# Zeroed tiles in one memset, shared K semaphores, a 16-slot last piece of V, and the final scale on VectorE, in a single-core decode attention kernel

## The chip, the cores and the metric

The kernel runs on one core of a Trainium2 chip. The metric is device time of one execution in microseconds (us), lower is better. The engines are called TensorE (PE in the profile), VectorE (DVE), ScalarE (ACT), GpSimd (POOL) and SyncE (SP); the last one issues nearly all the loads here. Unless a text says otherwise, a position is counted from the start of the profiled span; where several runs are compared in one table it is counted from the issue of the first load of K, which comes 0.95 to 0.96 us later.

## The reference

Single-token attention over a long cache: 32 query heads share 8 heads of K and V, each of 65536 keys by 128 values, all in bf16.

```
B, Hq, Hkv, Sq, Sk, D = 1, 32, 8, 1, 65536, 128
scores = einsum("bhqd,bhkd->bhqk", q, repeat(k, 4)) * D ** -0.5
p      = softmax(scores)
out    = einsum("bhqk,bhkd->bhqd", p, repeat(v, 4))
```

K and V together are 268 MB, and the output is 8 KB. Each byte is used once.

## The kernel before

For each of the G = 8 K/V heads, K and V come in two blocks of 256 "slots" (a slot is one key for each of 128 partitions: 32 KB). VectorE transposes K in place, TensorE makes the scores, ScalarE the exponentials, and TensorE multiplies them with V. The last block of V comes in pieces, at the slot numbers in CUTS.

```python
SL, TAIL, P, D, G, H = 256, 32, 128, 128, 8, 4
CUTS = [0, 128, 192, 224, 232, 240, 248, 252, 256]

def wait(self, *waits):              # Queue.wait, line 37 of the profile's listings
    for sem, n in waits:
        if n > 0:
            self.eng.wait_ge(sem, n)
...
    ex = sb("ex", [P, 4, 512], bf16)      # exponentials
    vs = sb("vs", [P, D + 2], fp32)       # sums that the last gather adds up over partitions
    vy = sb("vy", [P, D, 4], fp32)
...
    GP.mark(gp.memset(wz[:, :, :], 0.0))
    GP.mark(gp.memset(vs[:, :], 0.0))
    GP.mark(gp.memset(ex[:, :, :], 0.0))
    GP.mark(gp.memset(vy[:, :, :], 0.0))
    n = GP.mark(gp.memset(ident[:, :], 0.0))
...
    with block("pe_values"):              # V times exponentials, "wide": 512 columns a matmul
        take(pe, PE, s_et, 1)
        for ch in range(4):
            ...                           # waits for the load of this quarter
            for tt in range(16 if ch < 3 else (SL - TAIL) % PS // 4):
                i = wide(ch, tt)
            ...
            if ch in (1, 2):              # a matmul whose result nobody reads
                pe.matmul(out=pt[0:16, :], lhsT=et[:, 0, 0:16], rhs=et[:, 0, :],
                          start=True, stop=True)
...
    # the end on TensorE: 32 slots as "narrow" matmuls, 128 columns each
    for t in range(SL - TAIL, SL):
        if t in CUTS:
            pe.wait_ge(s_v[CUTS.index(t)], 16)
        if t == CUTS[-2]:
            pe.wait_ge(s_dv, d_last)
            gather(D, start=False, stop=False)      # adds VectorE's sums of all other slots
        w0 = t % PS // 4 * 32 + 16 + 4 * (t % 4)
        i = pe.matmul(
            out=fin, lhsT=et[:, 1, w0:w0 + H], rhs=io[:, t, :], start=(t == SL - TAIL),
            stop=(t == SL - 1), skip_group_check=True,
        )
    i.then_inc(s_pe, 1)
...
    # the end on VectorE and ScalarE
    n = DV.mark(dve.tensor_tensor(
        out=vs[:, 0:D], in0=vz[:, 0, :], in1=vz[:, 1, :], op=ALU.add
    ))
    assert n == d_last
    DV.wait((s_pt, 1))
    d_rl = DV.mark(dve.reciprocal(out=rl[:, :], in_=pl))
    ACTQ.wait((s_dv, d_rl), (s_pe, 1))
    n = ACTQ.mark(act.activation(out=o[:, :], in_=fin, func=ACT.Copy, scale=rl[:, :]))
    ACTQ.after(n)
    act.dma_start(out=out[0, (G - 1) * H:G * H, 0, :], in_=o[:, :]).then_inc(s_st, 16)
    ACTQ.wait((s_st, 32))
```

## Time and profile before

| | before |
|---|---|
| time, median of 3 | 629.61 us (629.51 to 629.65) |
| span of the profiled execution | 627.7 us |
| moved by DMA | 268.49 MB, 428 GB/s over the span |
| busy: TensorE, VectorE | 57%, 55% of the span |
| last piece of V has landed | 624.11 us |
| output DMA issued | 625.28 us |

The page's rows by slice: each digit is the busy share of one of 40 slices of 15.7 us in tenths, PEclk is the clock granted to TensorE in tenths of full speed, and GB/s is what the DMA moved.

```profile
PEclk9978595967959678596785958859587695899676
DMA  8999999999999999999999999999999999999996
GB/s 362 441 468 401 468 401 468 401 468 401 468 401 464 405 459 409 447 422 447 422 438 430 426 443 409 459 405 464 401 468 401 468 401 468 396 437 434 434 432 274
```

The DMA engines are busy at 90% or more in all slices but the first and the last. The kernel is a stream, and only its two ends can be shortened. TensorE's clock moves between half and full speed all the time: the clock record of this trace has 38 stretches at either 0.50 or 1.00, and the mean granted clock of the execution was 0.796.

The chain of waits that ended last, in order of time (start us, us, what; x is a count). Its end:

```profile
609.01 12.42 DMA io<-in_v_dram
621.43 0.04 issue
621.48 1.03 PE acc L254 x6
622.50 0.03 PE pb L348
622.53 1.80 PE pf L359 x28
624.33 0.23 PE pf L248 x2
624.56 0.24 PE pf L359 x4
...
624.82 0.02 ACTq L37
624.84 0.05 issue
624.89 0.36 ACT o L487
```

The chain names the piece of slots 192 to 223 as the last DMA. The trace's records of DMA completions show more: the pieces that begin at slots 192, 224, 232, 240, 248 and 252 had landed at 621.43, 622.11, 622.78, 623.45, 623.78 and 624.11 us. So the 28 narrow matmuls (L359) follow the landings closely, and the gather (L248) starts about when the last piece is there. After the last matmul (end 624.79 us) ScalarE waits (ACTq L37), and takes 0.36 us.

The startup, from the timeline (start us, us, engine, line, operation, out<-in):

```profile
1.52 0.21 POOL L187 MEMSET vs<- 128x130 f32 x1
1.67 1.81 POOL L188 MEMSET ex<- 128x2048 bf16 x1
3.41 0.52 POOL L189 MEMSET vy<- 128x512 f32 x1
...
8.50 4.45 DVE L373 STREAM_TRANSPOSE io<-io 128x4096 uint32<-128x4096 uint32 x1 [1.34 <-DVEq L119]
```

VectorE waits 1.34 us for the first K piece, after everything else of the startup is done.

### The profile page before, as it was taken

What the parts mean: (1) busy time and instruction counts of PE and PEld (TensorE: products, weight loads), DVE (VectorE), ACT (ScalarE), POOL (GpSimd) and SP (SyncE); (2) the same over time, 40 slices, a digit from 0 to 9 for tenths busy, and PEclk for the clock granted to TensorE, in tenths of its full rate; (3) what the DMA queues carried; (4) which work ended last, traced back from release to release, by engine and by line L of the source; (5) the groups of instructions that cost most, each with busy time, mean ns of one, the idle gap of its engine ahead of it and who ended that gap; (6) DMA issues with size and microseconds to landing.
All of it is one profiled execution on the core that took longest, in us unless ns stands there. A gap on an engine that the chain in (4) does not pass through costs nothing. (4 is left out here: it accounts for less than half of the span.)

```text
span 627.7 us, 7067 instructions
## 1 busy us (share of the span) xinstructions
PE 356.4 (57%) x2142; PEld 139.8 (22%) x2142; DVE 345.5 (55%) x154; ACT 34.4 (5%) x26; POOL 9.7 (2%) x42
## 2 busy tenths in 40 slices
PE   1865483827638275381844808458193571886346
PEld 0322131312213032130321303123031230332112
DVE  7795835649066490764807557084670946684210
ACT  0000100020000200002000020000200002000100
POOL 2000000000000000000000000000000000000000
PEclk9978595967959678596785958859587695899676
DMA  8999999999999999999999999999999999999996
GB/s 362 441 468 401 468 401 468 401 468 401 468 401 464 405 459 409 447 422 447 422 438 430 426 443 409 459 405 464 401 468 401 468 401 468 396 437 434 434 432 274
DMA packets 7003, 268.49 MB, mean 428 GB/s; under 512 B 856, under 2 KB 1112, under 8 KB 1496
## 3 DMA queue, kind: packets, MB, share of 16 engines
q1 hardware_dynamic: 6944, 268.45, 99.2%
q8 instruction: 1, 0.02, 0.0%
q14 instruction: 2, 0.02, 0.0%
q10 hardware_dynamic: 56, 0.01, 0.0%
HBM read 268.44 MB, written 0.01 MB: 428 GB/s over the span
## 5 line engine op out<-in xcount | busy, mean ns | idle before, releaser
L301 PE MATMUL acc<-io,wz 128*128 x1024 | 272.7, 420 | 184.8 <-PEq L119 157.3
L373 DVE STREAM_TRANSPOSE io<-io 128x4096 uint32<-128x4096 uint32 x64 | 279.9, 4416 | 157.2 <-DVEq L119 157.2
L301 PEld LDWEIGHTS acc<-io,wz 128*128 x1024 | 106.4, 104 | 351.2 <-issue 272.5
L254 PE MATMUL acc<-io,et 128*16 128x512 bf16 x1016 | 72.5, 416 | 19.3 <-PEq L119 19.2
L440 ACT ACTIVATE ex<-acc,nmb 128x2048 bf16<-128x2048 f32 x8 | 15.7, 1967 | 556.9 <-DVE nmb L420 556.9
L410 DVE TENSOR_REDUCE mg<-acc 128x1 f32<-128x2048 f32 x8 | 18.3, 2291 | 48.3 <-DVEq L119 48.3
L254 PEld LDWEIGHTS acc<-io,et 128*16 128x16 bf16 x1016 | 27.7, 94 | 58.4 <-issue 35.5
L248 PE MATMUL pf<-vs,sel 128*4 128x130 f32 (+1 forms) x20 | 5.7, 386 | 54.2 <-PEq L119 54.2
L376 DVE STREAM_TRANSPOSE et<-ex 128x1024 bf16<-128x1024 bf16 x17 | 20.8, 1225 | 22.6 <-SPq L154 12.8
L450 ACT ACTIVATE acc<-wz 128x2560 f32<-128x2560 bf16 (+2 forms) x8 | 16.3, 2040 | 1.0 <-ACT ex L440 0.2
L412 DVE TENSOR_REDUCE m<-pt 1x4 f32<-1x128 f32 x8 | 2.2, 279 | 22.7 <-DVEq L119 22.7
L514 POOL COPY wz<-qT 32x16 bf16<-32x16 bf16 x32 | 6.1, 189 | 512.6 <-PE acc L301 440.3
L248 PEld LDWEIGHTS pf<-vs,sel 128*4 128x4 f32 x20 | 1.2, 83 | 54.7 <-issue 54.6
L326 PE MATMUL pt<-et 128*16 128x512 bf16 x32 | 13.1, 411 | 0.0
L384 DVE TENSOR_REDUCE vs<-vy 128x128 f32<-128x512 f32 x9 | 6.1, 681 | 7.6 <-DVEq L119 7.6
L423 DVE TENSOR_TENSOR vy<-acc,sely 128x512 f32<-128x512 f32 x8 | 8.5, 1064 | 0.0
L472 DVE TENSOR_TENSOR vy<-acc,sely 128x512 f32<-128x512 f32 x1 | 0.7, 691 | 11.5 <-PE acc L254 11.5
L343 PE MATMUL pb<-ident,nrow 1*128 1x1 f32 x8 | 1.6, 194 | 7.5 <-PEq L119 7.5
L326 PEld LDWEIGHTS pt<-et 128*16 128x16 bf16 x32 | 3.1, 97 | 4.5 <-issue 1.4
L341 PE MATMUL pt<-ident,mg 128*1 128x128 f32 x8 | 2.3, 283 | 2.6 <-PEq L119 2.6
L420 DVE COPY nmb<-pb 128x1 f32<-128x1 f32 x8 | 1.3, 157 | 3.9 <-DVEq L119 3.9
L343 PEld LDWEIGHTS pb<-ident,nrow 1*128 1x128 f32 x8 | 1.1, 139 | 8.9 <-issue 8.9
(31 smaller groups left out, 22.8 us busy)
## 6 DMA issues: line engine op xcount, KB each, us to landing
io<-in_v_dram SPq DMA_DIRECT2D x5, 4096.0 KB, 16.9
io<-in_k_dram SPq DMA_DIRECT2D x8, 2048.0 KB, 27.4
io<-in_k_dram SPq DMA_DIRECT2D x2, 4096.0 KB, 34.4
io<-in_v_dram SPq DMA_DIRECT2D x1, 2048.0 KB, 10.3
io<-in_v_dram SPq DMA_DIRECT2D x1, 1024.0 KB, 12.4
io<-in_v_dram SPq DMA_DIRECT2D x3, 256.0 KB, 12.8
io<-in_v_dram SPq DMA_DIRECT2D x2, 128.0 KB, 12.8
io<-in_k_dram SPq DMA_DIRECT2D x13, 48.4
```

Of the source, the lines that this page charges most:

```text
L248: return pe.matmul(out=pf[0:H, 0:w], lhsT=sel[:, :], rhs=vs[:, 0:w], skip_group_check=True, **kw)
L254: return pe.matmul(out=vacc[32 * c:32 * c + 16, :, :], lhsT=et[:, ch // 2, w0:w0 + 16], rhs=io[:, PS * ch + 4 * tt:PS * ch + 4 * tt + 4, : ...
L301: i = pe.matmul(out=bass.AP(acc, r_o, [[2560, P], [1, 512]]), lhsT=bass.AP(wz, r_w + ((2 * s + e) * WB - 4 * u), [[4 * WB, P], [1, P]]), r ...
L326: pe.matmul(out=pt[0:16, :], lhsT=et[:, 0, 0:16], rhs=et[:, 0, :], start=True, stop=True)
L373: dve.transpose(out=part, in_=part).then_inc(s_kt, 2)
L376: dve.transpose(out=et[:, :, :].rearrange("p i n -> p (i n)"), in_=ex[:, 2 * b:2 * b + 2, :].rearrange("p i n -> p (i n)"),).then_inc(s_et, 1)
L384: DV.mark(dve.tensor_reduce(out=vs[:, 0:D], in_=vy[:, :, :], axis=AX.X, op=ALU.add))
L410: dve.tensor_reduce(out=mg[:, :], in_=sc, axis=AX.X, op=ALU.max).then_inc(s_mg, 1)
L423: dve.tensor_tensor(out=vy[:, :, :].rearrange("p d y -> p y d"), in0=vacc, in1=sely[:, :, None].to_broadcast([P, 4, D]), op=ALU.mult,).the ...
L440: act.activation(out=ex[:, :, :].rearrange("p b n -> p (b n)"), in_=sc, func=ACT.Exp, bias=nmb[:, :], scale=SCALE, accum_out=vs[:, D + g % ...
L450: act.activation(out=part, in_=wz[:, 0, 0:1].to_broadcast([P, part.shape[1]]), func=ACT.Copy).then_inc(s_cl, 1)
L514: gp.tensor_copy(out=wz[r, :, c0:c0 + H].rearrange("p (s w) h -> p s w h", s=2), in_=qTb[r, :, :, g, :],).then_inc(s_w, 1)
```

## The change

The intent is to trim both ends: fewer GpSimd instructions and waits at the start, one piece fewer at the end, and one engine fewer between the last product and the output, since VectorE has the reciprocal already. The sharing of K semaphores and the single allocation save resources more than time.

```diff
-CUTS = [0, 128, 192, 224, 232, 240, 248, 252, 256]
+CUTS = [0, 128, 192, 224, 240, 248, 252, 256]
...
-    ex = sb("ex", [P, 4, 512], bf16)
-    vs = sb("vs", [P, D + 2], fp32)
-    vy = sb("vy", [P, D, 4], fp32)
+    zs = sb("zs", [P, 1024 + 4 * D + D + 2], fp32)
+    ex = zs[:, 0:1024].bitcast(bf16).rearrange("p (b n) -> p b n", n=512)
+    vy = zs[:, 1024:1024 + 4 * D].rearrange("p (d y) -> p d y", y=4)
+    vs = zs[:, 1024 + 4 * D:]
...
     s_k = {(b, lo): sem(f"s_k{b}_{lo}") for b in range(2) for lo in k_lo}
+    for lo in k_lo[1::2]:
+        s_k[1, lo] = s_k[0, lo]
...
-    GP.mark(gp.memset(vs[:, :], 0.0))
-    GP.mark(gp.memset(ex[:, :, :], 0.0))
-    GP.mark(gp.memset(vy[:, :, :], 0.0))
+    GP.mark(gp.memset(zs[:, :], 0.0))
...
-    for s in (s_k[1, 64], s_k[1, 192]):
-        gp.sem_inc(s, 16 * (G - 1))
...
-    ACTQ.wait((s_dv, d_rl), (s_pe, 1))
-    n = ACTQ.mark(act.activation(out=o[:, :], in_=fin, func=ACT.Copy, scale=rl[:, :]))
-    ACTQ.after(n)
+    DV.after(d_rl)
+    DV.wait((s_pe, 1))
+    n = DV.mark(dve.tensor_scalar_mul(out=o[:, :], in0=fin, scalar1=rl[:, :]))
+    ACTQ.wait((s_dv, n))
     act.dma_start(out=out[0, (G - 1) * H:G * H, 0, :], in_=o[:, :]).then_inc(s_st, 16)
...
+            if g == 1:
+                GP.wait((s_sc, 8))
+                for t in k_lo[1::2]:
+                    gp.sem_inc(s_k[0, t], 16 * (2 * G - 2))
             GP.wait((s_sc, 16 * g))
             gp.sem_inc(s_sd, 1)
             if g == 1:
-                for t in k_lo[1:]:
-                    gp.sem_inc(s_k[0, t], 16 * (G - 1))
+                gp.sem_inc(s_k[0, 128], 16 * (G - 1))
```

## The prediction

> **What bounds the kernel now.** The DMA stream. The page moves 268.49 MB; the slice table shows the DMA engines at 90% or more in every slice but the first and the last, and the windows view gives 430 to 440 GB/s from 25 to 600 us, with DMA shares of 0.99 to 1.02. [...] PE (57%) and VectorE (55%) have slack. K loads land 48.4 us and V loads 29.4 us after issue (DMA issues), which is far more than the transfer of one 8.4 MB block (about 19.3 us), so the queue always has a next load: compute in the middle costs nothing. Outside the stream are about 2 us before the first packet and all after the last V landing (about 624.1 of 627.7 us).
>
> **Startup.** The three POOL memsets (0.21, 1.81, 0.52 us) become one of 1666 fp32 columns. From vy (512 columns, 0.52 us) and ident (128, 0.20 us) the slope is about 0.83 ns a column: about 1.5 us. The setup ends about 1 us earlier. Worth nothing: VectorE already idles 1.34 us before the first K transpose (start 8.50 us), which waits for the first K piece.
>
> **Shared K semaphores.** The credits of POOL for the second half of each K now come after the first block's scores. The second K block lands after about 32 us, when those scores are done (about 30 us): 0.
>
> **Last V pieces.** In the trace the pieces of slots 192, 224, 232, 240, 248 and 252 land at about 621.43, 622.11, 622.78, 623.45, 623.78 and 624.11 us. An 8-slot piece takes 0.67 us. Packets of 2 KB took 85 ns and of 8 KB 314, so by interpolation 4 KB takes about 161 ns against 2x85: each engine saves about 0.07 us, and the last piece lands about 0.08 us earlier. But TensorE must now wait for slot 224 until about 622.7 rather than 622.39. Its last 32 narrow matmuls run at 55.5 ns each at full clock (107 ns at the half clock granted before about 622.7). 28 of them from 622.75 end at about 624.3; before, the last gather of the sums started at 624.155. So TensorE, not DMA, becomes the last to arrive: +0.15 us (estimate).
>
> **Final scale.** ScalarE: product done 624.79, start 624.89, 0.358 us, output DMA issue 625.28. VectorE: the 4x130 copy from PSUM took 0.28 us and started 0.044 us after its matmul; the hop to ScalarE's queue costs about 0.04. Issue about 0.37 us after the product in place of 0.49: -0.13 us.
>
> **Sum.** +0.15 - 0.13 = about 0: 629.6 us, range 629.1 to 630.1, almost certainly within 2%.
>
> **What would show it.** One POOL memset of about 1.5 us; first K transpose still at 8.5 us; same GB/s in the middle; last piece landing at most 0.1 us earlier relative to the first load; an idle of TensorE of about 0.35 us before the final narrow matmuls, then 28 of them without a gap, and the gather later by 0.15 us; VectorE scale about 0.28 us.
>
> **What would make it wrong.** The half clock staying on through the last matmuls (28 x 50 ns = 1.4 us); a different stream rate in the middle, 0.1% of which is 0.6 us, more than everything argued here; a slow state.

## The result, and the profile after

| | before | after |
|---|---|---|
| time, median of 6 | 629.63 us (629.46 to 630.68) | 630.61 us (630.30 to 632.59) |
| ratio, 95% interval | | 1.0022 (1.0006 to 1.0038) |

The change was meant to shorten the kernel and made it 1.0 us longer by the medians, which is outside of the predicted range (629.1 to 630.1 us). The six times fall in two groups: 630.30, 630.53, 630.59 and 630.63 us, and 632.32 and 632.59 us. The profiled execution is the one of 632.32 us. Its slices, in the columns of before:

```profile
DMA  8999999999999999999999999999999999999995
GB/s 366 432 466 399 466 399 466 399 466 412 453 424 441 441 424 453 412 461 403 466 399 466 399 466 399 466 399 466 399 466 399 466 399 466 398 433 432 432 426 208
```

The stream is as full as it was. The difference is at the end. The chain after:

```profile
608.75 14.18 DMA io<-in_v_dram
622.93 0.04 issue
622.98 3.15 PE pf L359 x28
626.12 0.43 PE pf L248 x2
626.55 0.44 PE pf L359 x4
626.99 0.03 issue
627.02 0.02 DVEq L37
627.04 0.45 issue
627.49 0.34 DVE o L488
```

Two lines stand out. The 28 narrow matmuls take 3.15 us in one uninterrupted row, where before they took 1.80 us with waits between them. And after the separate wait of VectorE (DVEq L37) there are 0.45 us in which VectorE waits for nothing that the profile shows, where ScalarE had 0.05 us.

The windows view gives the reason for the first line. Columns: window, its length, busy us and count of each engine, then the granted TensorE clock, the DMA share and GB/s. Before:

```profile
623.00:624.00 1.00, 1.00 (x21) 0.93 (x18) 0.93 (x4) 0.00 (x0) 0.00 (x0) 1.00 0.26 70
```

After:

```profile
623.00:624.00 1.00, 1.00 (x11) 1.00 (x12) 0.93 (x3) 0.00 (x0) 0.00 (x0) 0.50 0.18 49
624.00:625.00 1.00, 1.00 (x12) 1.00 (x11) 0.31 (x2) 0.00 (x0) 0.00 (x0) 0.50 0.00 0
```

TensorE ran these matmuls at the half clock (0.50), 0.107 us from start to start where full clock gives 0.056 us. The prediction had named this as a risk. Which clock the end meets differs from one execution to the next: in the clock records of all 18 traces the changes lie on a grid of 3.41 us, and this grid begins 0.06 to 3.32 us after the first instruction (1.56 us in the trace of before, 3.05 us in that of after).

The startup did what was expected, to no avail:

```profile
1.52 1.49 POOL L191 MEMSET zs<- 128x1666 f32 x1
...
8.33 4.45 DVE L373 STREAM_TRANSPOSE io<-io 128x4096 uint32<-128x4096 uint32 x1 [2.10 <-DVEq L121]
```

The memset takes 1.49 us, VectorE is ready earlier, and it waits 2.10 us instead of 1.34 us for the same piece of K.

### The profile page after: what moved, and what is told of

It is laid out like the page before. It is cut to its first block, busy times and chain, and to the rows that moved or that the text cites. A ratio compares the mean times of both kernels' runs of the same rounds, so it can differ in the third digit from the quotient of the medians. Undisturbed runs are those within 1.5% of the kernel's fastest.

```text
span 630.5 us, 7062 instructions
## 1 busy us (share of the span) xinstructions
PE 352.6 (56%) x2142; PEld 139.7 (22%) x2142; DVE 345.8 (55%) x155; ACT 34.1 (5%) x25; POOL 8.8 (1%) x40
## 5 line engine op out<-in xcount | busy, mean ns | idle before, releaser
L301 PE MATMUL acc<-io,wz 128*128 x1024 | 268.3, 413 | 189.9 <-PEq L121 158.7
L301 PEld LDWEIGHTS acc<-io,wz 128*128 x1024 | 104.9, 102 | 353.4 <-issue 274.4
L440 ACT ACTIVATE zs<-acc,nmb 128x2048 bf16<-128x2048 f32 x8 | 15.7, 1967 | 556.8 <-DVE nmb L420 556.8
L248 PE MATMUL pf<-zs,sel 128*4 128x130 f32 (+1 forms) x20 | 6.0, 401 | 53.3 <-PEq L121 53.3
L376 DVE STREAM_TRANSPOSE et<-zs 128x1024 bf16<-128x1024 bf16 x17 | 20.8, 1225 | 22.0 <-SPq L158 12.2
L248 PEld LDWEIGHTS pf<-zs,sel 128*4 128x4 f32 x20 | 1.3, 88 | 53.7 <-issue 53.7
L384 DVE TENSOR_REDUCE zs<-zs 128x128 f32<-128x512 f32 x9 | 6.1, 681 | 7.6 <-DVEq L121 7.6
L423 DVE TENSOR_TENSOR zs<-acc,sely 128x512 f32<-128x512 f32 x8 | 8.5, 1065 | 0.0
L472 DVE TENSOR_TENSOR zs<-acc,sely 128x512 f32<-128x512 f32 x1 | 0.7, 690 | 12.5 <-PE acc L254 12.5
L359 PE MATMUL pf<-io,et 128*4 128x128 bf16 x32 | 3.8, 312 | 0.2 <-DMA io<-in_v_dram 0.2
L359 PEld LDWEIGHTS pf<-io,et 128*4 128x4 bf16 x32 | 3.3, 126 | 0.5 <-DMA io<-in_v_dram 0.3
```

The costliest lines, as they stand in the source:

```text
L248: return pe.matmul(out=pf[0:H, 0:w], lhsT=sel[:, :], rhs=vs[:, 0:w], skip_group_check=True, **kw)
L301: i = pe.matmul(out=bass.AP(acc, r_o, [[2560, P], [1, 512]]), lhsT=bass.AP(wz, r_w + ((2 * s + e) * WB - 4 * u), [[4 * WB, P], [1, P]]), r ...
L359: i = pe.matmul(out=fin, lhsT=et[:, 1, w0:w0 + H], rhs=io[:, t, :], start=(t == SL - TAIL), stop=(t == SL - 1), skip_group_check=True,)
L376: dve.transpose(out=et[:, :, :].rearrange("p i n -> p (i n)"), in_=ex[:, 2 * b:2 * b + 2, :].rearrange("p i n -> p (i n)"),).then_inc(s_et, 1)
L384: DV.mark(dve.tensor_reduce(out=vs[:, 0:D], in_=vy[:, :, :], axis=AX.X, op=ALU.add))
L423: dve.tensor_tensor(out=vy[:, :, :].rearrange("p d y -> p y d"), in0=vacc, in1=sely[:, :, None].to_broadcast([P, 4, D]), op=ALU.mult,).the ...
```

## The experiments

The theory after the result: three terms, all at the end. (i) The merged piece makes TensorE begin its narrow matmuls later, and it then has no slack left. (ii) VectorE begins the final multiply 0.45 us late. (iii) In some runs the half clock stretches the narrow matmuls. The rival: the code's place in memory moved (a guess, for the traces hold no addresses of the code), and an instruction fetch that shares a DMA engine with the stream is what delays the end. One of 8 KB came at 518 us before and at 615 us after, that is, inside the last pieces. One packet of the stream that starts as the fetch ends was slow in each trace: 2.77 us before, where the others of 64 KB took 2.42 to 2.52 us, and 0.96 us after, where the others of 16 KB in the last 30 us took 0.61 to 0.62 us. That the two shared an engine is inferred from this. Sixteen kernels were run in all, each with five timed rounds beside the kernel before (best_warm with a sixth run), and all gave correct results. Where an interval below contains 1, the times alone don't tell the two kernels apart. What tenths of a microsecond mean is therefore read from the traces, step by step, with one trace for each kernel.

### One part of the change at a time

Each of these is the kernel before with only the hunks of the diff above that its name says: the cut, the final scale, the zeroed allocation with its memset, or the semaphores.

```diff
 cuts_only:  -CUTS = [0, 128, 192, 224, 232, 240, 248, 252, 256]
             +CUTS = [0, 128, 192, 224, 240, 248, 252, 256]
 scale_only: -n = ACTQ.mark(act.activation(out=o[:, :], in_=fin, func=ACT.Copy, scale=rl[:, :]))
             +n = DV.mark(dve.tensor_scalar_mul(out=o[:, :], in0=fin, scalar1=rl[:, :]))   (and its waits)
 zs_only:    the allocation zs and its one memset
 sems_only:  the sharing of s_k and GpSimd's credits for it
```

> The old kernel with the merged 16-slot piece alone. Theory (two costs in the tail, merged piece and VectorE scale): the last 28 narrow matmuls start about 0.6 us later (after the whole 16-slot piece has landed) and then run without a gap, so +0.4 us in runs where TensorE is at full clock there (matmul pitch 0.055 us), and about +2 us in runs where the half clock (0.107 us) is granted. Rival (code layout: an 8 KB instruction fetch that moved into the last 15 us slows one DMA engine, and the pieces as such cost nothing): within 0.1 us of before.

> The old kernel with the final scale by VectorE alone. Theory: the VectorE multiply starts 0.4 to 0.5 us after the last matmul's end (ScalarE: 0.1 us) and takes 0.34 us (ScalarE: 0.36 us), so +0.35 to +0.4 us, the same in every run. Rival (that gap of 0.45 us in the changed kernel's trace was an accident of the half clock or of the fetch): start within 0.1 us, time -0.1 to 0.

> The old kernel with the one zeroed allocation and single memset alone. Theory: POOL's memsets 1 us shorter, first K transpose still at 8.3 to 8.5 us, time within 0.1 us of before. Rival (new addresses slow ScalarE's or VectorE's accesses or move the clock windows so that the tail is granted the half clock): +0.3 us or more, or a second group of runs over 1 us higher.

> The old kernel with the shared K semaphores alone. Theory: within 0.1 us of before; the second K block's transposes start when its data land (about 32.8 us), as before. Rival (instruction fetch moves): an 8 KB instruction fetch after 600 us and the last V piece's slowest sixteenth 0.3 us later, +0.2 us or more.

| | median | lowest to highest | ratio (95% interval) |
|---|---|---|---|
| before, same rounds | 629.52 us | 629.37 to 630.27 | |
| cuts_only | 629.66 us | 629.59 to 630.94 | 1.0004 (0.9991 to 1.0018) |
| scale_only | 630.46 us | 630.24 to 630.49 | 1.0012 (0.9998 to 1.0025) |
| zs_only | 629.73 us | 629.34 to 630.36 | 1.0000 (0.9987 to 1.0014) |
| sems_only | 629.48 us | 629.23 to 630.41 | 1.0001 (0.9987 to 1.0015) |

The allocation and the semaphores show nothing that stands out of before's own spread: zs_only's median is 0.2 us higher, but its lowest run is level with before's lowest. The final scale alone gives nearly the whole difference of the medians: all five of its runs lie between 630.24 and 630.49 us, and of the nine runs of before only the slowest (630.27 us) reaches that, although the interval of the ratio just contains 1. Its chain shows the 0.45 us again, now at full clock and with the old pieces:

```profile
624.70 0.24 PE pf L359 x4
624.93 0.03 issue
624.96 0.02 DVEq L37
624.98 0.45 issue
625.44 0.34 DVE o L488
```

So the gap belongs to the final scale and not to the half clock. Nor does it need the fetch that moved: in scale_only's trace that one comes at 516 us, far from the end, and the rival falls in the form stated. But the median is 0.94 us up, and the multiply explains only 0.40 us of it (the output DMA is issued 0.887 us after the last matmul's end, before: 0.491 us). Most of the rest comes after the issue: ScalarE sees the output landed 1.81 us after the issue, before 1.45 us. That was in no theory. (The last 0.14 us between the two traces is a last matmul that ends later.)

In cuts_only the narrow matmuls begin when the whole merged piece has landed, 0.51 us later than before, and run at full clock for most of the way, after about five at the half clock:

```profile
622.85 0.04 issue
622.90 1.97 PE pf L359 x28
624.86 0.22 PE pf L248 x2
```

The gather starts 0.52 us later than before, as the theory has it. The time is only 0.14 us up by the medians, because in this trace the output was seen 1.18 us after the issue, 0.27 us sooner than before. The same unknown term, with the other sign.

### What the 0.45 us is, and what delays the output

scale_tt is scale_only with the multiply written without a per-partition scalar operand. scale_late_end and before_late_end let VectorE's program end later. after_again repeats the changed kernel, for a trace of its faster group.

```diff
 scale_tt:
-    n = DV.mark(dve.tensor_scalar_mul(out=o[:, :], in0=fin, scalar1=rl[:, :]))
+    n = DV.mark(dve.tensor_tensor(
+        out=o[:, :], in0=fin, in1=rl[:, :].to_broadcast([H, D]), op=ALU.mult
+    ))
 scale_late_end (on scale_only) and before_late_end (on before):
     ACTQ.wait((s_st, 32))
+    DV.wait((s_st, 32))
```

> scale_only with the VectorE multiply written as tensor times tensor (the 1/l column broadcast along 128 columns), same waits, so that no per-partition scalar operand is read. Theory A (the scalar operand makes VectorE start late): the multiply starts about 0.1 us after the last matmul's end instead of 0.52 us, and the time falls by about 0.4 us against scale_only (630.46 us). Rival B (the gap comes from the two waits, or from a long-idle VectorE): start still at 0.5 us, no change against scale_only.

> scale_only with VectorE waiting for the output DMA before its program ends. Theory C (when VectorE's program ends, an 8 KB instruction fetch is issued that delays one of the four output packets' landings; with VectorE as the last engine it collides with the output): the fetch moves behind the output's landing, issue to landing falls from 1.79 us (slowest of four) to about 1.17 us as for the other three, time -0.4 to -0.6 us against scale_only. Rival D (the fetch is tied to another engine, or the slow fourth landing has another cause): fetch still about 1.2 us after the last matmul and no change.

> The old kernel with VectorE waiting for the output DMA before its program ends. Theory C: the slowest of the four output landings comes at 1.15 to 1.2 us after the issue in place of 1.42, time -0.2 to -0.3 us against before. Rival D: no change (within 0.1 us).

> The changed kernel again. Theory: two groups of times, about 630.5 us where the 28 narrow matmuls run at full clock (pitch 0.056 us) and about 632.4 us where the half clock is granted (0.107 us); two thirds or more in the first. In a full-clock trace the last matmul ends about 0.5 us later than in before, relative to the first load. Rival (the difference between 630.5 and 632.4 us has nothing to do with that clock): a 630.5 us trace shows the pitch of 0.107 us as well.

| | median | lowest to highest | ratio (95% interval) |
|---|---|---|---|
| before, same rounds | 629.85 us | 629.37 to 630.65 | |
| scale_tt | 631.08 us | 630.21 to 631.20 | 1.0017 (1.0003 to 1.0031) |
| scale_late_end | 630.50 us | 630.37 to 631.64 | 1.0015 (1.0001 to 1.0029) |
| before_late_end | 630.31 us | 629.97 to 630.91 | 1.0005 (0.9992 to 1.0019) |
| after_again | 630.60 us | 630.34 to 631.55 | 1.0017 (1.0004 to 1.0031) |

scale_tt clears the scalar operand: the multiply still starts 0.513 us after the last matmul's end (scale_only 0.518 us), although it is shorter (0.278 us against 0.337 us). Theory A falls. The trace is of the run of 630.21 us; three of the five runs took 631.08 to 631.20 us, and of these there is no trace.

before_late_end supports theory C where it applies: the 8 KB instruction fetch that before has 0.53 us after the last matmul now comes after the output's landing, and the output is seen 1.18 us after its issue instead of 1.45 us. Contrary to the expectation the kernel isn't faster for it: VectorE's end is now itself the last thing and costs about 0.5 us, and the traced run (630.91 us) also met the half clock. In scale_late_end, where VectorE also waits, the fetch stays at 1.19 us and the output at 1.67 us; the expected gain of 0.4 to 0.6 us did not come. So the fetch is not simply tied to the end of VectorE's program, which is what theory C had said; moving it still moved the output's landing with it.

after_again fell into the faster group in its profile, and the same program now shows the short pitch. Its chain:

```profile
622.95 0.04 issue
623.00 1.73 PE pf L359 x28
624.72 0.22 PE pf L248 x2
624.94 0.24 PE pf L359 x4
625.18 0.03 issue
625.21 0.02 DVEq L37
625.23 0.45 issue
625.68 0.34 DVE o L488
```

1.73 us for the same 28 matmuls against 3.15 us: this one difference of 1.4 us, with 0.41 us more for the gather and the last four (0.87 us against 0.46 us), covers the 1.8 us between the spans (630.5 and 628.7 us). The five times again fall in two groups, 630.34 to 630.60 us and 631.49 to 631.55 us. For the execution of 632.32 us no cause beyond the clock is thus needed. The slower group of after_again was expected at about 632.4 us, lies 0.8 us lower, and has no trace, so its cause is not shown. The kernel before can meet the half clock too: the trace of before_late_end shows a pitch of 0.107 us for nearly all of its narrow matmuls, with the old pieces.

### The order of the two waits

VectorE's multiply has two waits, and no arithmetic instruction in these traces carries more than one (of the 4506 in the trace of before 58 carry one, none carries two). The semaphores that the trace records show what becomes of the two: the first wait in the program (for the reciprocal) is the multiply's own, and the second (for the last matmul) stands before it as an instruction by itself. VectorE starts 0.45 us after that separate wait (after, after_again, scale_only). The trace of before has a wait for a matmul that VectorE's instruction carries itself, as its only one: the copy at 595.46 us starts 0.04 us after the matmul's end, having idled for 0.83 us. The guess was that the multiply, too, would start sooner if the late wait were the one that it carries. That makes a test without any other change:

```diff
 scale_swap (on scale_only):
-    DV.after(d_rl)
     DV.wait((s_pe, 1))
+    DV.after(d_rl)
     n = DV.mark(dve.tensor_scalar_mul(out=o[:, :], in0=fin, scalar1=rl[:, :]))
 scale_take (on scale_only; scr is a new tile of 4x1):
     DV.after(d_rl)
-    DV.wait((s_pe, 1))
+    DV.mark(dve.memset(scr[:, :], 0.0))
+    d_take(s_pe)
     n = DV.mark(dve.tensor_scalar_mul(out=o[:, :], in0=fin, scalar1=rl[:, :]))
 before_mid_end (on before):
     ACTQ.after(n)
+    DV.wait((s_ac, n))
 gather_first (on before):
         if t == CUTS[-2]:
             pe.wait_ge(s_dv, d_last)
             gather(D, start=False, stop=False)
+        if t in CUTS:
+            pe.wait_ge(s_v[CUTS.index(t)], 16)
         (and these two lines no longer before the gather)
```

> scale_only with its two waits in the other order, so that the wait for the last matmul is the instruction's own and the wait for the reciprocal is the separate one before it. Theory F (VectorE needs about 0.45 us from the end of a separate wait to the start of an instruction that carries a wait of its own[...]): multiply starts 0.05 to 0.1 us after the last matmul's end, output issued at 0.42 to 0.45 us (scale_only 0.89), and the time falls by about 0.4 us against scale_only, to 630.0. Rival G (VectorE is late for a reason that lies in its code's place or its long idle): start still at 0.5 us.

> scale_only with the wait for the reciprocal moved to a small VectorE memset in front, and the wait for the last matmul kept as a separate instruction before the multiply, which then has no wait of its own (as the loop's instructions have it, where the gap after a separate wait is 0.09 us). Theory F: start at 0.13 to 0.2 us after the last matmul's end. Rival G, or the separate wait at this place alone being the cause: start still at 0.5 us.

> The old kernel with VectorE waiting for ScalarE's product before its program ends. Theory C (an instruction fetch of VectorE's end shares a DMA engine with one of the four output packets): the fetch, 0.53 us after the last matmul in before, comes about 0.7 us later, after the output packets (1.25 to 1.31 us); slowest landing 1.17 us after the issue in place of 1.42; time -0.2 us. If the fetch comes at 0.9 to 1.2 us instead, it collides and the time is +0.2 us. Rival D: no change of issue to landing.

> The old kernel with the gather of the sums before the wait for the last 4-slot piece, not after it. Expected from the trace of before: VectorE's sums are ready 0.07 us before that piece lands, the gather occupies TensorE 0.22 us, so the last matmul ends 0.05 to 0.09 us earlier at full clock; time -0.1 to 0. If the last piece is not what the gather waits for, no change.

| | median | lowest to highest | ratio (95% interval) |
|---|---|---|---|
| before, same rounds | 629.51 us | 629.28 to 630.26 | |
| scale_swap | 629.58 us | 629.12 to 630.05 | 0.9997 (0.9983 to 1.0011) |
| scale_take | 630.06 us | 629.76 to 630.78 | 1.0007 (0.9994 to 1.0021) |
| before_mid_end | 629.41 us | 629.23 to 630.05 | 0.9999 (0.9985 to 1.0012) |
| gather_first | 629.48 us | 629.25 to 629.51 | 0.9996 (0.9983 to 1.0010) |

The chain of scale_swap:

```profile
625.01 0.24 PE pf L359 x4
625.25 0.02 issue
625.27 0.34 DVE o L488
```

The 0.45 us are gone. The multiply starts 0.04 us after the last matmul's end, and the output is issued at 0.41 us instead of 0.89 us. The scale on VectorE now costs nothing against ScalarE; the median fell by 0.88 us against scale_only's, in rounds whose medians of before differ by 0.01 us. That is more than the 0.4 us expected, because the output now lands sooner after its issue, too (1.18 us in place of 1.81 us). In scale_take the wait is still a separate instruction, but the multiply behind it has none of its own, and it starts after 0.08 us:

```profile
625.55 0.08 issue
625.63 0.34 DVE o L490
```

So the order of the two waits decides over the 0.45 us; neither VectorE's idle time (1.4 us in best, where the multiply still starts 0.04 us after the last matmul) nor the kind of multiply does. In all six traces with the multiply in this place and the old order the gap is 0.45 us. Which part of the combination costs it is not shown. scale_take changed two things at once: the multiply carries no wait, and the separate wait is of the kind that also lowers the semaphore again, as in the loop, while the one in scale_only just waits. In the loop of this kernel, where such a lowering wait stands before instructions without a wait, VectorE starts 0.09 us after it when it is free, even after more than 2 us of idling (23 times in the trace of before). A late wait of the plain kind before an instruction that carries none was not tried on VectorE. ScalarE's instruction before had a plain separate wait and a carried one and started 0.05 us after the separate one; but the wait it carried was for VectorE's semaphore, while VectorE's multiply carries one for VectorE's own. Whether that matters was not tried either, and why VectorE needs the time was not settled.

before_mid_end moved the fetch to 1.62 us after the last matmul, behind the output's packets, and the output landed 1.19 us after the issue instead of 1.45 us. The median shows no gain that can be told apart (629.41 against 629.51 us, expected 0.2 us). Nor does this pair alone prove theory C: in gather_first and cuts_only, where VectorE's end is as in before, the fetch came early by itself and the output took 1.18 to 1.19 us, too. The evidence is the whole set of traces (us; the fetch and the packets are counted from the last matmul's end; the last column is output issue to the landing as ScalarE sees it):

| | output issued | 8 KB fetch | last output packet | issue to seen |
|---|---|---|---|---|
| scale_swap | 0.41 | 0.09 to 0.42 | 1.22 | 1.18 |
| gather_first | 0.49 | 0.12 to 0.54 | 1.30 | 1.19 |
| cuts_only | 0.49 | 0.14 to 0.69 | 1.30 | 1.18 |
| after_swap | 0.41 | 0.34 to 0.91 | 1.22 | 1.51 |
| sems_only | 0.49 | 0.43 to 0.74 | 1.30 | 1.31 |
| best_warm | 0.41 | 0.45 to 0.88 | 1.22 | 1.40 |
| before | 0.49 | 0.53 to 1.02 | 1.30 | 1.45 |
| zs_only | 0.49 | 0.54 to 1.11 | 1.31 | 1.63 |
| scale_only | 0.89 | 1.19 to 1.74 | 1.94 | 1.81 |
| after_again | 0.89 | 1.18 to 1.54 | 1.75 | 1.66 |
| before_mid_end | 0.49 | 1.62 to 1.95 | 1.31 | 1.19 |
| scale_take | 0.52 | none | 1.33 | 1.19 |

The output is four packets. In scale_only three of them go out at 1.64 to 1.67 us and the fourth at 1.94 us, after the fetch has ended; the fourth landing is the late one. Where the fetch has ended by 0.7 us, comes after the packets, or is absent, the output needs 1.18 to 1.19 us (seven of the 18 traces, of which the table shows twelve). In the other eleven, where it ends between 0.74 and 1.74 us, the output needs 1.31 to 1.91 us (most in scale_tt), and the last completion record comes 0.90 to 1.04 us after the fetch's end in every one of them, also where the packets themselves go out as usual (zs_only, after_swap). So the landing follows the fetch's end. That the late packet shares a DMA engine with the fetch is an inference, for the trace as used here does not name the engine, and what sets off the fetch stays open.

gather_first was worth nothing that can be told apart, as expected (-0.1 to 0 us).

### The pieces put together, and a try at the clock

after_swap is the whole changed kernel with the waits swapped. best is the changed kernel with the old cuts, the swapped waits and the early gather. after_warm and best_warm add matmuls that nobody reads, where TensorE waits for loads, to try whether that keeps its clock up.

```diff
 after_swap (on the changed kernel): the swap of scale_swap
 best (on the changed kernel): old CUTS, the swap of scale_swap, the hunk of gather_first
 after_warm (on the changed kernel), best_warm (on best):
             if ch in (1, 2):
-                pe.matmul(
-                    out=pt[0:16, :], lhsT=et[:, 0, 0:16], rhs=et[:, 0, :], start=True, stop=True
-                )
+                for _ in range(9 if ch == 1 else 4):
+                    pe.matmul(
+                        out=pt[0:16, :], lhsT=et[:, 0, 0:16], rhs=et[:, 0, :], start=True, stop=True
+                    )
```

> The changed kernel with the two waits of the final VectorE multiply in the other order. Theory (the wait order costs 0.45 us and then the output collides with an instruction fetch, together about 0.9 us; the merged piece costs 0.4 us at full clock, more at the half clock): multiply starts 0.04 us after the last matmul, output issued at 0.41, median near 629.7 to 629.9 us (changed kernel 630.6), a slower group up to 2 us higher still there in some runs. Rival (the merged piece is the larger part): median stays above 630.3 us.

> The changed kernel with 11 more unneeded matmuls in every V block (8 more after the second quarter, 3 more after the third) where TensorE waits for loads. Theory (the slower group of the changed kernel is the half clock in the 28 narrow matmuls): TensorE is granted full clock in the tail of nearly all runs, narrow pitch 0.056 us in the trace, no run above about 630.9 us. Rival (the second group has another cause): runs at 631.5 us or above remain. If the unneeded work delays the stream, all runs are slower than 631 us.

> The changed kernel with the old piece cuts, the waits of the final multiply in the other order, and the gather before the last piece's wait. Theory: product to issue 0.41 us (before 0.49), gather 0.05 us earlier, and no fetch in the way: median 629.2 to 629.4 us, 0.1 to 0.3 us below before; a slower group of about 630.1 us in some runs. Rival (single parts do not add): equal to before or slower.

> best with the 11 unneeded matmuls per V block of after_warm. Theory: as best in its faster group, and no slower group: all runs between 629.0 and 629.6 us. Rival (the spread of best has another cause, or the extra work delays the tail): no narrower than best, or slower.

| | median | lowest to highest | ratio (95% interval) |
|---|---|---|---|
| before, same rounds | 629.50 us | 629.17 to 630.53 | |
| after_swap | 630.48 us | 629.52 to 630.85 | 1.0011 (0.9998 to 1.0024) |
| after_warm | 631.60 us | 631.33 to 632.10 | 1.0031 (1.0018 to 1.0044) |
| best | 629.87 us | 629.24 to 630.15 | 1.0000 (0.9987 to 1.0013) |
| best_warm | 631.83 us | 631.12 to 633.26 | 1.0036 (1.0024 to 1.0048) |

after_swap missed: its median lies above the expected 629.7 to 629.9 us and meets the criterion that had been set for the rival, that the merged piece is the larger part (above 630.3 us). Three of its five runs lie at 630.48 to 630.85 us, apart from its two lower runs (629.52 and 629.85 us). The traced run is the one of 629.85 us, at full clock, 0.75 us below the traced full-clock run of the changed kernel (630.60 us, after_again). Its trace has the multiply 0.04 us after the last matmul, the issue at 0.41 us against 0.89 us, and the output seen 1.51 us after the issue against 1.66 us; 0.48 and 0.15 us of the 0.75 us are thus in the steps that the swap touches. That the three slower runs met the half clock is likely, but they have no trace. So the share of the wait order is shown at full clock; which part is the larger in the median of many executions is not.

The warm variants missed. The mean granted clock was higher with the added matmuls (0.837 to 0.839 in after_warm's runs and 0.837 to 0.840 in best_warm's, 0.802 to 0.813 in the changed kernel's six and 0.799 to 0.810 in best's), and their traces do show the full-clock pitch of 0.056 us in the tail, but the work that nobody needs delayed the stream: the last piece landed 1.3 us later in after_warm than in after_again (624.59 against 623.32 us, from the first load's issue). So they prove nothing on the slower group, and this way of keeping the clock up cost more than it gained.

best missed its 629.2 to 629.4 us and is level with before. Its traced run (630.15 us) met the half clock for 20 of its narrow matmuls. Nothing here is a version that clearly beats the kernel before.

## Why the prediction was wrong

The steps, from the three traces, in us from the issue of the first load of K:

| | before (629.51) | after, full clock (630.60) | after, half clock (632.32) |
|---|---|---|---|
| slots 224 to 239 landed | 621.83 | 622.00 | 621.98 |
| first narrow matmul | 621.43 | 622.04 | 622.02 |
| last piece landed | 623.15 | 623.32 | 623.29 |
| gather starts | 623.23 | 623.60 | 624.96 |
| last matmul ends | 623.83 | 624.21 | 626.02 |
| final multiply starts | 623.93 | 624.73 | 626.54 |
| output DMA issued | 624.32 | 625.10 | 626.91 |
| output seen by ScalarE | 625.77 | 626.76 | 628.58 |

Point by point:

- **What bounds the kernel: right.** The stream is as it was (DMA share 0.99 to 1.02 in the windows of the middle, before and after). The mean from 25 to 600 us in the trace of before is 433 GB/s; the windows that read 440 GB/s also read a DMA share of 1.02, so they count too much by about as much.
- **Startup and semaphores: right**, both worth nothing. zs_only and sems_only stayed within the spread of before. One detail was luck: the scores of the first block are done at 32.9 us in the trace of before and at 32.7 us in sems_only, not at about 30 us, and so only about when the first part of the second block lands (32.8 and 32.6 us). It cost nothing: the transposes of that part begin 0.13 to 0.14 us after the landing in both.
- **"+0.15 us" for TensorE in the last pieces: right in mechanism; the landings were mis-sized.** At full clock the gather starts 0.37 us later and the last matmul ends 0.38 us later. The mis-sized term is when the merged piece lands. The prediction had it 0.08 us before the second of the two old pieces; in the two traces of the changed kernel those slots came 0.15 and 0.17 us later than before, in after_swap and cuts_only 0.05 and 0.07 us later. The last piece of all landed 0.04 to 0.17 us later in these four traces, not 0.08 us earlier, but kernels with the old cuts also spread from 623.09 to 623.68 us, so this much is within what the stream does by itself. Counted from the landing of the last piece, which takes that out, the last matmul ends 0.89 to 0.90 us later in the two traces of the changed kernel at full clock (after_again, after_swap), and 0.65 to 0.68 us later in those with the old cuts at full clock or nearly so. The merged piece itself thus costs about 0.22 us at full clock, and the prediction's 0.15 and 0.08 us add up to the same 0.23 us. At the half clock the last matmul ended 2.73 us after the last landing (after), with the old cuts and most narrow matmuls at the half clock 1.66 us (before_late_end).
- **"Final scale: -0.13 us": wrong, and the step that failed.** "Issue about 0.37 us after the product in place of 0.49" became 0.89 us. The duration was a little low (0.28 us taken from a copy, 0.34 us measured). What failed is the start: the 0.044 us was read from an instruction whose only wait was for its matmul (the copy at 595.46 us), while this one stands behind a separate wait and carries another; it starts 0.52 us after the product. scale_swap brought this to 0.04 us by nothing but the order of the two waits.
- **That nothing changes after the output's issue** was left unsaid in the prediction and assumed in its sum ("about 0"). The issue moved by 0.40 us, but the end of the instruction fetch moved by 0.52 us (1.02 to 1.54 us after the last matmul), and the landing went with it: 1.66 us from issue to landing instead of 1.45 us, another 0.21 us.
- **"The half clock staying on": right as a risk, not weighed in the range.** It hit the profiled execution and made it 1.8 us longer than the full-clock one. The range of the prediction had no room for it. It is not what moved the median of the six runs, for that lies between two of the four runs near 630.5 us, and the one traced execution there (630.60 us) was at full clock.

The sum at full clock: 0.38 us (later end of the matmuls) + 0.40 us (scale) + 0.21 us (output) = 0.99 us, which is the difference of the two spans, 628.7 and 627.7 us.

## What to carry to other kernels

When an instruction on VectorE has several waits, look in the trace which of them it carries itself, and try to give it the one that comes last; here that was worth 0.48 us. Before changing the pieces at the end of a stream, count the slack of the engine that works behind it: a piece that is twice as large hands the work over in one lump, and what was hidden between landings then stands at the end, at whatever clock TensorE has just been granted (here the last matmul ended 0.89 to 0.90 us after the last landing at full clock, 2.73 us at the half clock). Moving one small operation also moved an instruction fetch here (the output's issue by 0.40 us, the fetch's end by 0.52 us), and the output took 0.21 us longer from issue to landing, so a step that is "unchanged" has to be read from the new trace too.
